# A chunked recurrence with a block-row solver in place of a power-series solver, followed by a capacity-dropping expert layer

## The chip, the cores and the metric

The kernel runs on one core of one Trainium2 chip, in one launch. The metric is device time in microseconds (us), the median of several runs; lower is better. Before the change it is 1976.67 us, the median of 3 runs (1975.95 to 1977.36).

## The reference

```python
# attention: batch 4, heads 8, tokens 768, head size 40, all float32
for t in range(S):
    y[:, :, t] = einsum('bhd,bhde->bhe', r_t, state)
    Sa = einsum('bhde,bhe->bhd', state, a_t)
    state = state * w_t[:, :, None, :] - einsum('bhd,bhe->bhde', Sa, b_t)
    state = state + einsum('bhd,bhe->bhde', v_t, k_t)
# experts: x = y as (3072 tokens, 320); 8 experts, hidden 1024, capacity 80
expert = argmax(x @ w_gate); gate = softmax(x @ w_gate)[expert]
for e in range(8):        # an expert keeps the 80 tokens with the greatest gates
    out[tok] = gate[tok] * (relu(x[tok] @ w1[e]) @ w2[e])
```

## The kernel before

Part 1 is the recurrence. Each token decays the state by w, so with P the running product of w from a start point, G = S / P obeys a recurrence without decay: G_t = G_{t-1} + v_t kh_t' + u_t nb_t', u_t = G_{t-1} ah_t, with ah = a times the product before t, kh = k / P, nb = -b / P. Within a stretch of tokens the u are the solution of a triangular system, U = (I - N)^-1 (ah G_0 + Psi V).

A unit is 128 tokens of one batch with all 8 heads; there are 24 units (6 chunks of 128 tokens times 4 batches). Two heads share 128 partitions, padded from 40 to 64 each. Inside a unit the products restart every 32 tokens (C = 32, NS = 4 sub-chunks); the masks `before` and `after` are block-diagonal in 32 tokens.

`prepare(n)` does what needs no state: six loads on the SP queue (`load`), transposes through TensorE (`transposed`, L180), the running product on VectorE (L225), its reciprocal (L229), the products N, its transpose, Psi and Lambda (`scores`, L192 with the mask at L199), and the inverse. The inverse is the product (I + N)(I + N^2)(I + N^4)(I + N^8)(I + N^16): a `while` loop multiplies z by a factor on TensorE (L264 by way of L192) and adds it on VectorE (L267), and squares N and its transpose (`power`, L192, copied by ScalarE at L208). `finish(n)` does what needs the state: for each of 4 sub-chunks a transposed copy of the state (L305), u (L309, L311), and the state step (L318, L320, L323, L324); then Lambda of u, y (L340 to L349), the token rows of x and the logits.

`together(finish(n), prepare(n + 1))` takes a step of each in turn, so the two generators' instructions alternate in each engine's queue. Each engine runs its queue in order; a framework places the instructions and puts semaphores between engines.

An f32 matmul stands in the trace as two passes, each a weight load and a MATMUL; a transpose is one pass. After every fourth unit `gate` picks experts and merges the greatest gates with 10 rounds of MAX8 and MATCH_REPLACE8 on VectorE. Part 2 (L429 on) finds each expert's tokens and runs the 8 experts; it starts when part 1 ends.

Of the kernel before, what the change touches and what calls it, by code (L numbers as in the profile page):

```python
# [8 lines left out]
F32 = mybir.dt.float32  # L9
# [4 lines left out]
Alu = mybir.AluOpType  # L14
PSUM = bass.MemoryType.PSUM
# [3 lines left out]
def kernel(  # L19
# [57 lines left out]
    def keep(o, i, op, base, pattern, cm):  # L77
# [18 lines left out]
    own = const.tile([128, 1, 1, 2], F32, name="own")
    nc.vector.memset(own, 0.0)
    nc.vector.memset(own[0:HB, :, :, 0:1], 1.0)
    nc.vector.memset(own[HB:128, :, :, 1:2], 1.0)
    # E, E - 1, ... 1: the greatest of those at the maxima is the first maximum  # L100
# [4 lines left out]
    # a tile m = (ci, batch) holds tokens batch * S + ci * T + p; one more than that  # L105
# [31 lines left out]
    with ExitStack() as p1:  # L137
        hold = p1.enter_context(tc.tile_pool(name="hold", bufs=1))
        sb = p1.enter_context(tc.tile_pool(name="sb", bufs=2))
        ps_t = p1.enter_context(tc.tile_pool(name="ps_t", bufs=2, space=PSUM))  # L140
        ps_s = p1.enter_context(tc.tile_pool(name="ps_s", bufs=2, space=PSUM))
        ps_c = p1.enter_context(tc.tile_pool(name="ps_c", bufs=2, space=PSUM))
# [7 lines left out]
        src = dict(w=w, a=a, k=k, b=b, r=r, v=v)  # L150
        raw = {n: padded(f"raw_{n}", 3 if n == "v" else 2, [128, H, HB], 1.0 if n == "w" else 0.0) for n in src}
        decay = padded("decay", 2, [128, G * NS, C], 0.0)
        u_t = padded("u", 2, [128, H, HB], 0.0)
        state = [padded(f"state{i}", 2, [128, G, 2, HB], 0.0) for i in range(B)]
# [7 lines left out]
        def given(name, n):  # L162
            return raw[name][n % len(raw[name])]

        def load(n):
            if n >= len(units):
                return
            ci, bi = units[n]
            for name, ap in src.items():
                nc.sync.dma_start(given(name, n)[:, :, 0:D],  # L170
                                  ap[bi, :, ci * T : (ci + 1) * T, :].rearrange("h t d -> t h d"))
# [4 lines left out]
        def transposed(t, n=G):  # L176
# [6 lines left out]
        def per_head(lhs, rhs, n=128):  # L183
            """A product per head, heads of parity q in bank q: index (q, g)."""
            p = ps_s.tile([128, 2, 512], F32, name="sp", tag="s")
            for g in range(G):
                for q in range(2):
                    o = p[:, q, g * n : (g + 1) * n]
                    x = rhs(q, g)
                    if len(x.shape) == 3:  # L190
                        o = o.rearrange("p (s d) -> p s d", s=x.shape[1])
                    nc.tensor.matmul(o, lhsT=lhs(q, g), rhs=x, start=True, stop=True)  # L192
            return p

        def scores(lhs, rhs, mask, tag, bufs):
            p = per_head(lambda q, g: lhs[HB * q : HB * q + D, g, :],
                         lambda q, g: rhs[HB * q : HB * q + D, g, :])
            o = sb.tile([128, 2, G, 128], F32, name=tag, tag=tag, bufs=bufs)
            nc.vector.tensor_tensor(  # L199
                out=o.rearrange("p q g t -> p (q g) t"), in0=p.rearrange("p q (g t) -> p (q g) t", g=G),  # L200
                in1=mask.to_broadcast([128, H, 128]), op=Alu.mult)
            return o

        def power(x, y, tag):
            """The square of y, of which x is the transpose."""
            p = per_head(lambda q, g: x[:, q, g, :], lambda q, g: y[:, q, g, :])
            o = sb.tile([128, 2, G, 128], F32, name=tag, tag=tag, bufs=2)
            nc.scalar.copy(o.rearrange("p q g t -> p q (g t)"), p)  # L208
            return o

        def flat(t):
            return t.rearrange("p g t -> p (g t)")

        ready = {}

        def prepare(n):
            """What needs no state, in steps."""
            rw = {name: given(name, n) for name in src}

            # running products of w, tokens along the free axis  # L220
            wp = transposed(pairs(rw["w"])).rearrange("p g (c t) -> p (g c) t", c=NS)
            dec = decay[n % 2]
            nc.scalar.copy(dec[:, :, 1:C], wp[:, :, 0 : C - 1])
            Ee = sb.tile([128, G * NS, C], F32, name="Ee", tag="Ee")
            nc.vector.tensor_tensor_scan(flat(Ee), flat(dec), flat(begins), 0.0, op0=Alu.mult, op1=Alu.add)  # L225
            Pp = sb.tile([128, G * NS, C], F32, name="Pp", tag="Pp", bufs=1)
            nc.vector.tensor_tensor(out=Pp, in0=wp, in1=Ee, op=Alu.mult)
            iP = sb.tile([128, G, 128], F32, name="iP", tag="iP", bufs=1)
            nc.vector.reciprocal(flat(iP), flat(Pp))  # L229
# [358 lines left out]
```

## Time and profile before

| | |
|---|---|
| median of 3 runs | 1976.67 us |
| profiled execution, span | 1975.8 us |
| TensorE matmul busy | 1795.4 us (91%) |
| VectorE, ScalarE, GpSimd busy | 670.5, 350.4, 32.3 us |
| mean granted TensorE clock | 0.790 |

The profiled execution's own time is its span: the first instruction starts at 0 and the last ends at 1975.8. The granted clock is a share of full speed (2.4 GHz); it has two levels, 1.0 and 0.5, so 0.79 is a mix of both in time. PE is TensorE, PEld its weight loads, DVE VectorE, ACT ScalarE, POOL GpSimd; SPq is a queue that issues DMAs. A bracket in a timeline row says how long the engine idled before the row and what released it.

### The profile page before, as it was taken

The numbers are of one execution on the slowest core, as the hardware profiler recorded it, in microseconds if no ns is written. First come the engines' busy times: TensorE is split into PE (matmuls) and PEld (weight loads), VectorE is DVE, ScalarE is ACT, GpSimd is POOL, SyncE is SP. The second block draws the span as 40 slices with busy tenths as digits, with TensorE's granted clock in tenths as the row PEclk, the third lists the DMA queues.
The fourth block names the chain that finished last, engine by engine and source line by source line (L and its number), as shares of the span: only waits on it lengthen the run. The fifth ranks groups of instructions, "written<-read, shape, count | busy, mean of one in ns | idle before, by whom it ended". The sixth has DMA issues, their size and how long they took to land. (4 is left out here: it accounts for less than half of the span.)

```text
span 1975.8 us, 28976 instructions
## 1 busy us (share of the span) xinstructions
PE 1795.4 (91%) x13014; PEld 1603.5 (81%) x13014; DVE 670.5 (34%) x1203; ACT 350.4 (18%) x503; POOL 32.3 (2%) x81
## 2 busy tenths in 40 slices
PE   4899999899999899999899999899999899982998
PEld 3798898798889789889789889789889888872766
DVE  4323323523332532332532332532332532316000
ACT  0221121121121121121121121121122112110000
POOL 1000000000000000000000000000000000000100
PEclk9886897797797797797697788788788689765677
DMA  8100100100110110110110110110110100005330
GB/s 190 17 5 17 21 8 14 34 14 11 17 21 4 31 21 4 18 21 4 31 21 4 18 21 4 31 21 4 18 21 5 34 4 1 1 1 175 121 117 7
DMA packets 168494, 55.95 MB, mean 28 GB/s; under 512 B 150964, under 2 KB 165556, under 8 KB 168372
## 3 DMA queue, kind: packets, MB, share of 16 engines
q1 hardware_dynamic: 160896, 44.58, 11.0%
q10 hardware_dynamic: 6708, 7.89, 1.2%
q8 instruction: 103, 1.69, 0.3%
q0 software_dynamic: 768, 1.64, 0.3%
q14 instruction: 19, 0.16, 0.0%
HBM read 45.40 MB, written 8.70 MB: 27 GB/s over the span
## 5 line engine op out<-in xcount | busy, mean ns | idle before, releaser
L192 PE MATMUL sp<-z,Nt 128*128 128x80 f32 x1920 | 281.4, 308 | 1.8 <-ACT Nt L208 1.2
L192 PEld LDWEIGHTS sp<-z,Nt 128*128 128x128 f32 x1920 | 261.9, 219 | 16.8 <-issue 6.4
L192 PE MATMUL sp<-Nt,Nn 128*128 128x128 f32 x1536 | 228.3, 311 | 0.0
L192 PEld LDWEIGHTS sp<-Nt,Nn 128*128 128x128 f32 x1536 | 217.6, 226 | 0.0
L208 ACT COPY Nt<-sp 128x1024 f32<-128x1024 f32 x96 | 97.2, 1012 | 489.9 <-PE sp L192 489.9
L318 PE MATMUL cp<-raw_v,kh 32*128 32x80 f32 x736 | 171.4, 318 | 0.0
L267 DVE TENSOR_TENSOR z<-sp,z 128x320 f32<-128x320 f32 x240 | 106.6, 486 | 189.9 <-PE sp L192 189.9
L320 PE MATMUL cp<-u,nb 32*128 32x80 f32 x736 | 165.7, 310 | 3.9 <-DVE u L311 3.9
L323 DVE TENSOR_TENSOR acc<-cp,state 128x320 f32<-128x320 f32 x92 | 43.9, 477 | 313.0 <-PE cp L320 313.0
L318 PEld LDWEIGHTS cp<-raw_v,kh 32*128 32x128 f32 x736 | 132.7, 223 | 17.2 <-issue 11.9
L192 PE MATMUL sp<-Nn,Nt 128*128 128x128 f32 x1152 | 141.2, 276 | 0.0
L305 ACT COPY sd<-tp 128x512 f32<-128x512 f32 x96 | 56.4, 587 | 478.7 <-PE tp L180 477.2
L320 PEld LDWEIGHTS cp<-u,nb 32*128 32x128 f32 x736 | 134.2, 225 | 5.0 <-DVE u L311 4.8
L192 PEld LDWEIGHTS sp<-Nn,Nt 128*128 128x128 f32 x1152 | 135.9, 194 | 0.0
L311 DVE TENSOR_TENSOR u<-cp,z 32x320 f32<-32x320 f32 x96 | 46.7, 486 | 215.0 <-PE cp L309 214.9
L192 PE MATMUL sp<-ahT,nbT 40*128 40x128 f32 x384 | 49.9, 437 | 65.7 <-DVE nbT L240 65.7
L309 PE MATMUL cp<-state,zT 128*32 128x80 f32 x768 | 108.0, 291 | 0.0
L340 PEld LDWEIGHTS tp<-rT,sd 128*128 128x128 f32 x768 | 96.3, 197 | 12.8 <-issue 12.8
L340 PE MATMUL tp<-rT,sd 128*128 128x32 f32 x768 | 104.4, 281 | 0.0
L192 PEld LDWEIGHTS sp<-ahT,nbT 40*128 40x128 f32 x384 | 42.8, 324 | 72.4 <-DVE nbT L240 72.4
L309 PEld LDWEIGHTS cp<-state,zT 128*32 128x32 f32 x768 | 74.0, 139 | 31.2 <-issue 30.3
L542 PE MATMUL hp<-xe,w 128*128 128x80 f32 (+1 forms) x384 | 87.6, 374 | 1.4 <-DVE xe L534 1.4
(181 smaller groups left out, 2054.5 us busy)
## 6 DMA issues: line engine op xcount, KB each, us to landing
w<-in_moe_w_dram SPq DMA_DIRECT2D x8, 1280.0 KB, 8.8
w<-in_moe_w_dram SPq DMA_DIRECT2D x8, 1024.0 KB, 5.6
x_rows<-xb ACTq DMA_DIRECT2D x6, 642.0 KB, 4.2
out_dram<-zero ACTq DMA_DIRECT2D x8, 480.0 KB, 5.5
raw_w<-in_w_dram SPq DMA_DIRECT2D x24, 160.0 KB, 3.2
raw_a<-in_a_dram SPq DMA_DIRECT2D x24, 160.0 KB, 3.5
raw_k<-in_k_dram SPq DMA_DIRECT2D x24, 160.0 KB, 3.3
raw_b<-in_b_dram SPq DMA_DIRECT2D x24, 160.0 KB, 3.2
```

The lines of the kernel that those rows point to most:

```text
L192: nc.tensor.matmul(o, lhsT=lhs(q, g), rhs=x, start=True, stop=True)
L208: nc.scalar.copy(o.rearrange("p q g t -> p q (g t)"), p)
L267: nc.vector.tensor_tensor(out=zq, in0=p[:, q, 0 : G * 2 * D].rearrange("p (g s d) -> p g s d", g=G, s=2), in1=zq, op=Alu.add)
L305: nc.scalar.copy(sd, transposed(old.rearrange("p g q d -> p g (q d)")))
L309: nc.tensor.matmul(pu[tt, 2 * g : 2 * g + 2, :], lhsT=zT[:, g, tt], rhs=old[:, g, :, 0:D], start=True, stop=True)
L311: nc.vector.tensor_tensor(out=u[tt, :, 0:D], in0=pu[tt], in1=z[tt, 1, :, 0:D], op=Alu.add)
L318: nc.tensor.matmul(pg[:, g], lhsT=pairs(kh)[tt, g, :], rhs=rv[tt, h2, 0:D], start=True, stop=False)
L320: nc.tensor.matmul(pg[:, g], lhsT=pairs(nb)[tt, g, :], rhs=u[tt, h2, 0:D], start=False, stop=True)
L323: nc.vector.tensor_tensor(out=acc, in0=pg, in1=old[:, :, :, 0:D], op=Alu.add)
L340: nc.tensor.matmul(yp[:, g, tt], lhsT=starts[c][:, g, :], rhs=rT[:, g, tt], start=c == 0, stop=False, skip_group_check=True)
L542: nc.tensor.matmul(hp[:, f - f0, :], lhsT=w1[:n, i, f * 128 : (f + 1) * 128], rhs=xe[:n, i, :], start=i == 0, stop=i == len(KB) - 1)
```

## The change

The running products now run over all 128 tokens, and there is one state per batch, stepped once per unit. The system of 128 tokens is solved by block rows of 32: row c subtracts what the earlier rows contribute (L298), and multiplies by the inverse of its own diagonal block (L302). The 32x32 diagonal blocks of four units (4 batches x 4 blocks x 8 heads = 128 matrices) are written to DRAM, read back with one matrix in each partition, inverted there on VectorE by 30 steps of two instructions, written to DRAM and read back as weights (`invert`, once per four units). Preparation runs 5 units ahead, and the generators are gone: `finish(n)` is written out whole, then `prepare(n + 5)`. The products that divide b and k by P, and two of the masks, go to GpSimd (POOL). `gate` and part 2 stay as they are; comments are gone, so line numbers shift.

```diff
-        def power(x, y, tag):          # squares, ScalarE copies
-            while j < C:               # five factors, z += N^j z
-            for c in range(NS):        # in finish: 4 state steps a unit
-        together(finish(n, xb, lg), prepare(n + 1))
+        def by_pool(p, o):
+            nc.scalar.copy(o.rearrange("p q g t -> p (q g t)"), p.rearrange("p q g t -> p (q g t)"))
+            oo = o.rearrange("p q g t -> p (q g) t")
+            nc.gpsimd.affine_select(out=oo, in_=oo, compare_op=Alu.is_gt, fill=0.0, base=0,
+                                    pattern=[[0, H], [1, 128]], channel_multiplier=-1)
+        def prepare(n):
+            load(n, early)
+            nc.scalar.copy(dec[:, :, 1:], transposed(pairs(raw_w)))
+            nc.vector.tensor_tensor_scan(flat(pt), flat(dec), flat(begins), 0.0, op0=Alu.mult, op1=Alu.add)
+            nc.vector.scalar_tensor_tensor(out=ahT, in0=transposed(pairs(raw_a)), scalar=-1.0,
+                                           in1=pt[:, :, 0:T], op0=Alu.mult, op1=Alu.mult)
+            nc.vector.reciprocal(ip, heads(transposed(pt[:, :, 1:])))
+            nc.gpsimd.tensor_tensor(out=ub[:, :, 0:D], in0=raw_b[:, :, 0:D], in1=ip, op=Alu.mult)
+            nc.gpsimd.tensor_tensor(out=kh[:, :, 0:D], in0=raw_k[:, :, 0:D], in1=ip, op=Alu.mult)
+            ubT = copied("ubT", pairs(ub))
+            by_vector(scores(ubT, ahT), nt)
+            for c in range(NS):
+                nc.sync.dma_start(blocks[k, bi, c].rearrange("h (s t) -> s h t", s=C),
+                                  nt[tt].rearrange("p q g t -> p (q g) t")[:, :, tt])
+        def invert(k):
+            nc.sync.dma_start(lt, blocks[k].rearrange("b c h x -> (b c h) x"))
+            nc.scalar.copy(tt, lt)
+            for s in range(1, C - 1):
+                n = C - 1 - s
+                nc.vector.tensor_tensor(
+                    out=tm, in0=t3[:, 0:s, s : s + 1].to_broadcast([128, s, n]),
+                    in1=l3[:, s : s + 1, s + 1 :].to_broadcast([128, s, n]), op=Alu.mult)
+                nc.vector.tensor_tensor(out=t3[:, 0:s, s + 1 :], in0=t3[:, 0:s, s + 1 :], in1=tm, op=Alu.add)
+            nc.sync.dma_start(solved[k].rearrange("b c h x -> (b c h) x"), tt)
+            for bi in range(B):
+                for c in range(NS):
+                    nc.sync.dma_start(dt_[c * C : (c + 1) * C].rearrange("p q g t -> p (q g) t"),
+                                      solved[k, bi, c].rearrange("h (s t) -> s h t", s=C))
+        def finish(n, xb, lg):
+            by_pool(scores(copied("khT", pairs(kh), 1), ahT), lam)
+            by_pool(scores(vT, rT), lamv)
+            ...
+            for c in range(NS):
+                for h in range(H if c else 0):
+                    nc.tensor.matmul(pr[tt, h, :], lhsT=nt[0 : c * C, h % 2, h // 2, tt], rhs=u[0 : c * C, h, 0:D],
+                                     start=False, stop=True, skip_group_check=True)
+                nc.scalar.copy(yy[tt], pr[tt])
+                for h in range(H):
+                    nc.tensor.matmul(pu[tt, h, :], lhsT=dt_[tt, h % 2, h // 2, :], rhs=yy[tt, h, :],
+                                     start=h == 0, stop=True, skip_group_check=True)
+                nc.vector.tensor_copy(u[tt, :, 0:D], pu[tt])
+            ...
+        for ci in range(NCI):
+            for bi in range(B):
+                finish(n, xb, lg)
+                if m < len(units):     # m = n + AHEAD, 5
+                    prepare(m)
+                    if m % B == B - 1:
+                        invert(m // B)
```

On TensorE, in the middle of a unit before the change, the squares and factors of the next unit (Nt, Nn, z) stand between the steps of this one (u, sd, lamv, rT):

```order
L192 MATMUL sp<-Nt,Nn 128x128 x8
L180 MATMUL tp<-ident,u_144 128x128 x4
L340 MATMUL tp<-rT,sd 128x32 x4
L344 MATMUL tp<-lamv,kh 64x128
L192 MATMUL sp<-rT,uT 128x128 x8
L192 MATMUL sp<-z,Nt 128x80 x8
L346 MATMUL tp<-lamu,nb 64x128
```

After the change, the same place in a unit holds the last two of that unit's block rows (pu from dt, pr from nt) and then its end:

```order
L302 MATMUL pu<-yy,dt 32x40 x8
L298 MATMUL pr<-u_164,nt 32x40 x8
L302 MATMUL pu<-yy,dt 32x40 x8
L311 MATMUL pg<-u_164,ub_152 64x80 x8
L182 MATMUL tp<-ident,u_164 128x128 x4
L328 MATMUL yp<-rT,gT 128x128 x3
L196 MATMUL sp<-rT,uT 128x128 x8
L328 MATMUL yp<-rT,gT 128x128
L333 MATMUL yp<-lamv,kh_140 64x128 x8
L333 MATMUL yp<-lamu,ub_152 64x128 x8
L182 MATMUL tp<-ident,xT 128x128 x4
```

What stood between a unit's dependent steps there, another unit's matmuls, is no longer in that place.

On TensorE, at the seam between two units before the change, the preparation (raw_b, raw_k, nbT, ahT, khT) has state steps of the running units (u, nb, state, zT) among it:

```order
L320 MATMUL cp<-u_143,nb 128x80
L180 MATMUL tp<-ident,raw_b_126 128x128 x4
L180 MATMUL tp<-ident,raw_k_122 128x128 x4
L192 MATMUL sp<-ahT,nbT 128x128 x8
L192 MATMUL sp<-nbT,ahT 128x128 x8
L180 MATMUL tp<-ident,state_156 128x128 x4
L309 MATMUL cp<-state_156,zT 32x80 x4
L192 MATMUL sp<-ahT,khT 128x128 x8
```

After the change the end of a unit (xT, lp) is followed by the preparation of the unit five later (raw_w to ub_156), and that by the start of the next unit (kh_140):

```order
L182 MATMUL tp<-ident,xT 128x128 x4
L341 MATMUL lp<-wg,xT 128x8 x4
L182 MATMUL tp<-ident,raw_w_112 128x128 x4
L182 MATMUL tp<-ident,raw_a_116 128x128 x4
L182 MATMUL tp<-ident,pt 128x128 x4
L182 MATMUL tp<-ident,ub_156 128x128 x4
L182 MATMUL tp<-ident,kh_140 128x128 x4
L196 MATMUL sp<-ahT,ubT 128x128 x8
L196 MATMUL sp<-ahT,khT 128x128 x8
L182 MATMUL tp<-ident,raw_r_128 128x128 x4
```

The transposes that wait for the running product (pt) and its reciprocal (ub) now stand one behind the other, with one group of transposes (raw_a) before the first and none between the two.

On VectorE before the change, a unit's u and end (lamu) stand among the next one's factors (z):

```order
L311 TENSOR_TENSOR u_144<-cp,z 32x8x40
L267 TENSOR_TENSOR z<-sp,z 128x4x2x40 x2
L323 TENSOR_TENSOR acc<-cp,state_160 128x320
L324 TENSOR_TENSOR state_159<-acc,ends 128x8x40
L267 TENSOR_TENSOR z<-sp,z 128x4x2x40 x2
L199 TENSOR_TENSOR lamu<-sp,before 128x1024
```

After the change, the last steps of an inverse (tmp, tt) stand between the gate's rounds (MAX, MATCH_REPLACE on cand), in front of the next unit's u:

```order
L256 TENSOR_TENSOR tmp<-tt,lt 128x58
L378 MAX cand_180<-cand_179 128x8
L259 TENSOR_TENSOR tt<-tt,tmp 128x29x2
L379 MATCH_REPLACE cand_179<-cand_180,cand_179 128x208
L256 TENSOR_TENSOR tmp<-tt,lt 128x30
L378 MAX cand_180<-cand_179 128x8
L259 TENSOR_TENSOR tt<-tt,tmp 128x30
L379 MATCH_REPLACE cand_179<-cand_180,cand_179 128x208
L304 COPY u_163<-pu 32x8x40 x4
L315 TENSOR_TENSOR acc<-pg,state_167 128x320
```

The inverse of units 4k to 4k+3 ends right before unit 4k starts on its block rows.

## Rows read from the trace of the kernel before

**Rows 1.** The page, part 1: busy us, share of the span, instructions.

```profile
PE 1795.4 (91%) x13014; PEld 1603.5 (81%) x13014; DVE 670.5 (34%) x1203; ACT 350.4 (18%) x503; POOL 32.3 (2%) x81
```

**Rows 2.** Stretches: length, busy and count of PE, PEld, DVE, ACT, POOL; clock, DMA.

```profile
310.20:381.90 71.70, 66.46 (x506) 60.22 (x505) 30.49 (x72) 13.93 (x21) 0.68 (x3) 0.81 0.11 24
445.90:473.30 27.40, 24.12 (x135) 22.09 (x136) 11.23 (x15) 1.76 (x3) 0.00 (x0) 0.51 0.08 13
1747.00:1785.00 38.00, 32.31 (x164) 27.59 (x164) 5.69 (x11) 2.77 (x5) 0.00 (x0) 0.50 0.00 0
1798.00:1976.00 178.00, 149.52 (x591) 107.86 (x589) 25.85 (x71) 7.00 (x16) 14.96 (x16) 0.65 0.36 113
```

**Rows 3.** Timeline of one unit's preparation: start, us, engine, line, idle before.

```profile
449.18 2.08 PE L192 MATMUL sp<-ahT,nbT 40*128 40x128 f32 x16 [3.54 <-DVE nbT L240]
```

**Rows 4.** Timeline, last unit of part 1 alone on TensorE.

```profile
1747.07 1.09 PE L180 MATMUL tp<-ident,state 128*128 128x128 f32 x4 [1.27 <-DVE state L324]
1748.08 1.28 PE L309 MATMUL cp<-state,zT 128*32 128x80 f32 x8
...
1765.61 1.75 PE L340 MATMUL tp<-rT,sd 128*128 128x32 f32 x8
...
1767.91 2.08 PE L192 MATMUL sp<-rT,uT 40*128 40x128 f32 x16
...
1774.22 0.70 PE L344 MATMUL tp<-lamv,kh 128*64 128x128 f32 x4
1774.70 0.65 PE L346 MATMUL tp<-lamu,nb 128*64 128x128 f32 x4
...
1782.87 1.72 PE L357 MATMUL lp<-wg,xT 128*128 128x8 f32 x8
```

**Rows 5.** Groups by line and form: busy us, mean ns; idle before, releaser.

```profile
L192 PE MATMUL sp<-z,Nt 128*128 128x80 f32 x1920 | 281.4, 308 | 1.8 <-ACT Nt L208 1.2 <-DVE z L260 0.7
L318 PE MATMUL cp<-raw_v,kh 32*128 32x80 f32 x736 | 171.4, 318 | 0.0
L208 ACT COPY Nt<-sp 128x1024 f32<-128x1024 f32 x96 | 97.2, 1012 | 489.9 <-PE sp L192 489.9
L229 DVE RECIPROCAL iP<-Pp 128x512 f32<-128x512 f32 x24 | 80.2, 3340 | 0.0
L311 DVE TENSOR_TENSOR u<-cp,z 32x320 f32<-32x320 f32 x96 | 46.7, 486 | 215.0 <-PE cp L309 214.9
L199 DVE TENSOR_TENSOR lamu<-sp,before 128x1024 f32<-128x1024 f32 x24 | 29.4, 1224 | 104.5 <-PE sp L192 104.5
L225 DVE TENSOR_TENSOR_SCAN Ee<-decay,begins 128x512 f32<-128x512 f32 x24 | 29.3, 1220 | 15.1 <-ACT decay L223 15.1
L394 DVE MAX8 cand<-cand 128x8 f32<-128x208 f32 x60 | 21.7, 361 | 0.8
L349 DVE TENSOR_TENSOR xT<-tp,Ee 128x512 f32<-128x512 f32 x24 | 16.6, 691 | 119.5 <-PE tp L346 119.5
L331 ACT COPY uT<-tp 128x512 f32<-128x512 f32 x24 | 14.2, 592 | 2.4 <-PE tp L180 2.4
L354 ACT COPY xb<-tp 128x320 f32<-128x320 f32 x24 | 10.2, 426 | 55.4 <-PE tp L180 55.4
```

**Rows 6.** The same of GpSimd alone.

```profile
L232 POOL TENSOR_TENSOR ends<-Pp,own 128x32 f32<-128x32 f32 x24 | 5.7, 239 | 1327.3 <-DVE Pp L227 1327.3
...
L78 POOL TENSOR_SCALAR_AFFINE_SELECT strict<-ones 128x128 f32<-128x128 f32 x1 | 0.3, 282 | 0.0
```

**Rows 7.** Timeline of TensorE at the program's start.

```profile
21.38 1.08 PE L180 MATMUL tp<-ident,raw_w 128*128 128x128 f32 x4 [21.38 <-DMA raw_w<-in_w_dram]
...
38.05 3.61 PE L258 MATMUL cp<-raw_v,psi 128*128 128x40 f32 x16 [0.33 <-issue]
```

**Rows 8.** The page, part 6: DMA issues, KB each, us to landing.

```profile
out_dram<-zero ACTq DMA_DIRECT2D x8, 480.0 KB, 5.5
```

**Rows 9.** Timeline of VectorE where part 1 ends.

```profile
1784.62 0.17 DVE L358 COPY lg<-lp 128x8 f32<-128x8 f32 x1 [2.72 <-PE lp L357]
```

More of the change, by code (lines that the diff above doesn't have):

```diff
@@ L148, in padded @@
             return ts
[L150 to L154, printed above, removed]
+        early = dict(w=w, a=a, k=k, b=b)
+        late = dict(r=r, v=v)
+        raw = {n: padded(f"raw_{n}", 2, [128, H, HB], 1.0 if n == "w" else 0.0) for n in (*early, *late)}
+        decay = padded("decay", 2, [128, G, T + 1], 0.0)
+        khs = padded("kh", NK, [128, H, HB], 0.0)
+        ubs = padded("ub", NK, [128, H, HB], 0.0)
+        us = padded("u", 2, [128, H, HB], 0.0)
+        state = padded("state", B, [128, G, 2, HB], 0.0)
         og_t = padded("og", 2, [128, B, 32], 0.0)
@@ L181, in transposed, with copied, scores @@
             return p
-        def per_head(lhs, rhs, n=128):
-            p = ps_s.tile([128, 2, 512], F32, name="sp", tag="s")
+        def copied(name, t, bufs=2):
+            o = sb.tile([128, G, 128], F32, name=name, tag=name, bufs=bufs)
+            nc.scalar.copy(o, transposed(t))
+            return o
+        def scores(lhs, rhs):
+            p = ps_s.tile([128, 2, G, 128], F32, name="sp", tag="s")
             for g in range(G):
                 for q in range(2):
[L188 to L192, printed above, removed]
-            return p
@@ L204, in power @@
-        def power(x, y, tag):
[L206 to L214, printed above, removed]
+                out=o.rearrange("p q g t -> p (q g) t"), in0=p.rearrange("p q g t -> p (q g) t"),
+                in1=before.to_broadcast([128, H, 128]), op=Alu.mult)
@@ L226, in prepare @@
[L226 to L229, printed above, removed]
-            ends = sb.tile([128, NS, G, 2], F32, name="ends", tag="ends")
-            nc.gpsimd.tensor_tensor(
-                out=ends, op=Alu.mult, in1=own.to_broadcast([128, NS, G, 2]),
-                in0=Pp[:, :, C - 1 : C].rearrange("p (g c) o -> p c g o", c=NS).to_broadcast([128, NS, G, 2]))
@@ L243, in prepare @@
-            nc.vector.tensor_tensor(out=khT, in0=transposed(pairs(rw["k"])), in1=iP, op=Alu.mult)
-            yield
-            Nt = scores(nbT, ahT, before, "Nt", 2)
-            Nn = scores(ahT, nbT, after, "Nn", 2)
-            yield
-            psi = scores(khT, ahT, before, "psi", 1)
-            z = sb.tile([128, 2, H, HB], F32, name="z", tag="z")
-            nc.scalar.copy(z[:, 0].rearrange("p (g q) d -> p g (q d)", q=2), transposed(ahT))
-            yield
-            pv = ps_c.tile([128, H, D], F32, name="cp", tag="c")
@@ L292, in finish @@
         def finish(n, xb, lg):
             ci, bi = units[n]
-            Eg, ends, z, zT, kh, nb, rT, lamv = ready.pop(n)
-            rv = given("v", n)
-            u = u_t[n % 2]
-            starts = []
+            pt, ahT, ub, kh, nt = made.pop(n)
+            dt_ = inverse.pop((ci, bi))
+            load(n, late)
+            rr, rv = raw["r"][n % 2], raw["v"][n % 2]
+            st = state[bi]
+            lam = sb.tile([128, 2, G, 128], F32, name="psi", tag="psi", bufs=1)
+            by_pool(scores(copied("khT", pairs(kh), 1), ahT), lam)
@@ new lines, in finish @@
+            lamu = sb.tile([128, 2, G, 128], F32, name="lamu", tag="lamu", bufs=1)
+            by_vector(scores(copied("uT", pairs(u), 1), rT), lamu)
+            yp = ps_t.tile([128, G, 128], F32, name="yp", tag="t")
+            for g in range(G):
+                nc.tensor.matmul(yp[:, g, :], lhsT=gT[:, g, :], rhs=rT[:, g, :],
+                                 start=g == 0, stop=False, skip_group_check=True)
+            for x, y in ((kh, lamv), (ub, lamu)):
+                for g in range(G):
+                    for q in range(2):
+                        nc.tensor.matmul(yp[HB * q : HB * (q + 1), g, :], lhsT=x[:, 2 * g + q, :], rhs=y[:, q, g, :],
+                                         start=False, stop=x is ub, skip_group_check=True)
@@ L356, in finish @@
+            xT = sb.tile([128, G, 128], F32, name="xT", tag="xT")
+            nc.vector.tensor_tensor(out=xT, in0=yp, in1=pt[:, :, 0:T], op=Alu.mult)
+            nc.scalar.copy(xb[:, bi, 0:DM].rearrange("p (h d) -> p h d", h=H), heads(transposed(xT)))
+            lp = ps_t.tile([128, E], F32, name="lp", tag="t")
             for g in range(G):
```

208 lines of the change are left out of this document (79 added, 129 removed).

## The prediction, made before the changed kernel ran

> **What bounds the kernel now.** I read the page first. TensorE is busy for 91% of the span, in 13014 passes; VectorE and ScalarE are far below [rows 1]. So I asked for a table of stretches. A unit of part 1 takes 71.7 us, holds 506 recorded passes, and TensorE is busy 66.5 us of it, at a mean clock of 0.81 [rows 2]. The reader is to see that the bound is TensorE's own work, and that its price has two levels: 27.4 us of each period run at half clock (1.2 of 2.4 GHz) and hold 135 passes, about 0.2 us each [rows 2]. The timeline shows what comes before the fall: TensorE idles 3.54 us, until VectorE has the reciprocal and the product behind it [rows 3]. The last unit of part 1 has no other unit beside it. It shows how a unit runs alone: from 1747 to 1785 TensorE is busy 32.3 of 38 us, with gaps such as 1.27 us, and the clock is 0.50 throughout [rows 2, 4]. That stretch is my model of the changed kernel. Part 1 ends with the last logits at 1784.8 [rows 9]; what follows takes 1975.8 - 1784.8 = 191 us and is not changed.
>
> **What goes.** The power series goes: 5 factors and 7 squares of 8 matmuls each, 12 x 8 x 2 = 192 passes a unit. So do 3 of 4 state steps and transposed states. By the order, a unit has 320 passes afterwards (40 transposes; 64 of scores; 16 + 8 + 32 + 64 + 48 + 8 + 32 + 8 others), against the 506 recorded before. At the old mean price this alone would take the unit from 71.7 to 71.7 x 320/506 = 45 us. But the other unit that stood between dependent steps goes too, so a unit costs its chain of waits, and I price the chain.
>
> **Which clock.** The seam has two idle stretches per unit. The transposes of w and a take 1.8 us, while the decay copy and the scan need 0.6 + 1.2 us behind the first [rows 5], so TensorE idles about 1.3 us. Then it waits for the reciprocal of 320 columns, 3.34 x 320/512 = 2.1 us [rows 5], and for GpSimd's product, about 3 us in all. Waits of 3.5 and of 1.3 us stood before half-clock stretches in the trace [rows 3, 4]. I price all of part 1 at half clock.
>
> **Prices at half clock.** A transpose is 0.22 us (1.09 for four with 0.2 of latency at the end), a score pass 0.117 (2.08 for 16), a pass with 128 columns of weights 0.21 to 0.22 (L340, L357, L258), a pass with 64 columns 0.105 (eight from 1774.22 to 1775.35, less 0.3 of latency) [rows 4, 7]. A hand-over between engines is 0.05 to 0.15.
> No row has a pass of 32 columns of weights and 40 columns of data (L302, L298; 112 a unit). The nearest is L309: 32 columns of weights, 80 of data, 1.28 us for 8, which is 0.28 + 7 x 0.14 [rows 4]. If the data columns set it, half of them give 0.07; if not, 0.14. I take 0.09, nearer the half, and 1.6 us for 16.
> A rule weighs on this term. Contracting 32 rows instead of 128 buys nothing in the rows: 318 ns for L318 against 308 for z [rows 5]. The Trainium skill, TensorE: Matmul & The Clock Gate, section "Why this matters for your kernels", says the same, and that small blocks gain only when they run beside each other in different tiles of the array; here each block row waits for the one before. By that rule the block height buys nothing and 0.14 would stand, which is the second rival below.
> GpSimd has no row of these sizes. A select over 1024 columns lies between ScalarE's copy of as many, 1.0 us, and 8 x 0.282 = 2.3 [rows 5, 6]; taking 0.1 as its fixed part I use 1.5. A product of 320 columns lies between VectorE's 0.49 and 0.1 + 320 x (0.239 - 0.1)/32 = 1.5 [rows 5, 6]; I use 0.8.
> The Trainium skill, GPSIMD Engine Reference, section "Elementwise — side-by-side cycle accounting", has two-input work there about twice as slow as on VectorE. By that the product would be an estimated 0.97 us and the sum 4 us more.
>
> **One unit, in four parts.**
> A, preparation: transposes of w 1.1, decay copy 0.6, scan 1.25, transposes of pt 1.1, reciprocal 2.1, GpSimd 0.8, transposes of ub and kh 1.8, two groups of scores 3.9, hand-overs 0.5: 13.1 us.
> B, to the right-hand side: copy 1.0 and select 1.5 with hand-overs, 2.75 (three groups of transposes, 2.6, lie under it); 2 passes of L286 0.44; scores 1.86; 14 passes 3.1; 8 of L289 1.76; latency 0.3: 10.2 us.
> C, block rows: kh.v, which the order puts ahead of the first L302, 1.5; four L302 6.4; three L298 4.8; four copies of u 2.0 and three of yy 1.3 [rows 5]; eleven hand-overs 1.3: 17.3 us.
> D, end: ub.u 1.5, transposes 0.9, six passes of L328 1.3, scores 1.86, two more and 32 passes of L333 with latency 4.1, xT 0.85, transposes 1.1, logits 1.76: 13.4 us. VectorE's state step and lamu (1.22) lie under L333.
> Sum: 54 us. TensorE's share in it is 42 (the same prices over its 320 passes), so the chain is the bound. The last four units have no preparation and no state step: 39.5 us each.
>
> **The inverse.** 60 VectorE instructions, 9920 columns in all. VectorE takes 0.486 us for 320 and 1.224 for 1024 [rows 5], so 0.15 + 1.05 ns a column: 9.0 + 10.4, say 20 us. It is hidden only as far as a unit lasts. In order, its last 21 steps (6.2) alternate with the gate's 20 (at MAX8's 0.361 [rows 5], with their loads 8.0) and stand behind nt and before the next u: 15.5 us with overhead. Then the matrices go out, for which I take the 5.5 us of a 480 KB store [rows 8], and 32 KB pieces come back, 0 to 5.5, I take 3. So 24 us lie between nt and the first L302, where the other path needs 12: 12 us of stall, four times; the fifth time there is no preparation as cover, and it is 19. Sum: 67 us. SP issues the returning pieces in order behind the store, and later loads of r, v, w stand behind them; those are two units ahead, and cost nothing while the stall stays below a unit.
>
> **The start.** The first transposes come at 21.4 [rows 7]. Four preparations, each 9.5 behind the last, the last one whole: 42. Out to DRAM 3, back 5.5 (bounds as above), copy 1, inverse 20 with nothing beside it, out and back 8.5: first block row at 101. Chain and end of unit 0: 29.
>
> **Sum.** 101 + 29 + 19 x 54 + 4 x 39.5 + 67 + 191 = 1572. It is made against the profiled span of 1975.8, 0.9 under the median; I predict **1570 us**.
>
> **Rivals.**
> 1. The clock comes back in each unit's dense end (scores and L333, 7 us without a wait). For it: the clock does return in every period of the trace, after 27 us [rows 2]. Against it: that return follows dense full-width matmuls, and D is followed at once by the idle seam. D and what is left of A at full clock save about 6 us a unit: 1572 - 23 x 6 = 1430. If the clock stays up through most of part 1, a unit is about 37 us, and the time 1200.
> 2. Small passes cost 0.14: 112 x 0.05 = 5.6 us a unit, 24 times: 1705. For it the K = 32 rows above; against it the fewer data columns.
> 3. The other side: small passes do not follow each other closely, because all eight of a group stand in one 32x32 corner of the array and write one strip of PSUM. One pass alone has 0.28 to 0.3 of latency; unpipelined, 112 x (0.31 - 0.09) = 25 us a unit, 24 times 590: 2160, slower. It decides from 404/(24 x 112) = 0.15 us above my price, 0.24 a pass. Against it: L309 and L318 pipeline [rows 4, 5].
> 4. The inverse decides: at the price of 320 columns each, 60 x 0.486 = 29 us, 9 more at the start and in each stall: 1572 + 54 = 1625, inside my range.
>
> **How the numbers follow.** My sum 0.50, rival 4 0.06, rival 1 0.20 (its strong form 0.04 more), rival 2 0.15, rival 3 0.04, unnamed 0.01. Range 1430 to 1710: it holds the sum, rivals 2 and 4 and most of rival 1. A measurement of this kernel tells about 0.2%, 4 us, from no change. Faster 0.95, same 0.01, slower 0.04, the last from rival 3.
>
> **What would show it.** Right: clock near 0.5 over part 1; units about 54 us apart; TensorE's idle time named by GpSimd, VectorE's reciprocal and the u and yy copies; groups of L302 at 1.6 us; before units 4, 8, 12, 16, 20 a wait for dt of 12 to 19 us. Wrong: a clock above 0.7 in part 1; L302 groups at 2.4 us or at 5; no wait for dt, or one that outlasts a unit.

## The result, and the profile after

The changed kernel takes 1302.35 us (median of four runs, 1299.19 to 1305.5) against 1976.31 for the kernel before, run beside it: a ratio of 0.659, 95% interval 0.658 to 0.660. The forecast was 1570 us with a range of 1430 to 1710. The direction is right, the size is not: the gain is 674 us where 407 were forecast. The profiled execution has a span of 1303.7 us. Medians and ranges, here and below, leave out executions more than 1.5% above the fastest of their kernel: 1308.0 and 1314.4 us with all waits filled, 1542.1 in the interleaved kernel with the same fills, 1385.4 in the changed kernel with wider data, and 4166.1 in the kernel before, run beside that one.

The first part of the page, to be read beside [rows 1], and the row of the granted clock:

```profile
PE 958.8 (74%) x8150; PEld 815.8 (63%) x8150; DVE 440.5 (34%) x1015; ACT 211.0 (16%) x365; POOL 128.2 (10%) x179
...
PEclk9966775668566767775677656675765567557777
```

TensorE's passes fall from 13014 to 8150 and its share of the span from 91% to 74%: it now waits in every unit, as foreseen. But its clock in part 1 is not 0.5; it moves between 0.5 and 0.8. Next the stretches, as in [rows 2]: two whole units (5 and 6, counting from 0), then the four parts of unit 7: preparation, right-hand side, block rows, end.

```profile
301.40:343.20 41.80, 32.45 (x320) 28.64 (x320) 10.31 (x14) 8.19 (x14) 4.06 (x5) 0.71 0.16 28
343.20:390.10 46.90, 38.12 (x320) 33.54 (x320) 10.32 (x13) 8.19 (x14) 4.06 (x5) 0.56 0.14 25
390.10:402.40 12.30, 7.51 (x53) 6.49 (x54) 5.31 (x4) 1.76 (x3) 1.68 (x2) 0.69 0.32 55
402.40:409.00 6.60, 6.60 (x54) 6.13 (x56) 0.00 (x0) 3.75 (x5) 2.18 (x2) 0.81 0.48 124
409.80:421.40 11.60, 8.15 (x114) 7.00 (x114) 3.76 (x12) 2.30 (x4) 0.15 (x1) 0.58 0.09 16
421.40:431.50 10.10, 8.75 (x88) 7.65 (x88) 8.20 (x23) 1.01 (x2) 0.22 (x1) 0.80 0.01 2
```

A unit holds the 320 passes that were counted from the order, and lasts 42 to 47 us, not 54. Both units do the same work; the one of 46.9 us had the lower clock, 0.56 against 0.71. Inside unit 7 the clock is low in the preparation and the block rows, where TensorE is busy 61% and 70% of the time, and high in the right-hand side and the end (100% and 87%). The timeline of TensorE shows the turns:

```profile
390.13 0.66 PE L182 MATMUL tp<-ident,raw_w 128*128 128x128 f32 x4 [0.26 <-DVE lg L342]
...
392.73 0.66 PE L182 MATMUL tp<-ident,pt 128*128 128x128 f32 x4 [1.51 <-DVE pt L223]
396.64 1.12 PE L182 MATMUL tp<-ident,ub 128*128 128x128 f32 x4 [3.25 <-POOL ub L230]
...
398.54 2.08 PE L196 MATMUL sp<-ahT,ubT 40*128 40x128 f32 x16
400.41 1.92 PE L196 MATMUL sp<-ahT,khT 40*128 40x128 f32 x16
...
405.18 1.16 PE L196 MATMUL sp<-rT,vT 40*128 40x128 f32 x16
...
409.79 0.76 PE L302 MATMUL pu<-yy,dt 32*32 32x40 f32 x16
...
412.39 1.27 PE L302 MATMUL pu<-yy,dt 32*32 32x40 f32 x16 [0.51 <-ACT yy L300]
414.24 1.27 PE L298 MATMUL pr<-u,nt 64*32 64x40 f32 x16 [0.57 <-DVE u L304]
...
426.73 1.09 PE L333 MATMUL yp<-lamv,kh 128*64 128x128 f32 x16
...
460.28 0.97 PE L302 MATMUL pu<-yy,dt 32*32 32x40 f32 x12 [6.29 <-DMA dt<-solved]
```

Four transposes take 0.66 us ahead of the wait of 3.25 us and 1.12 behind it; sixteen score passes take 2.08 at half clock, and 1.16 after 8 us of work without a wait. A group of sixteen small passes takes 0.76 us at full clock and 1.27 at half. The last row is the wait for the diagonal inverse, in unit 8. Eight us without a wait do not always bring the clock back. In unit 6 the same passes run without a wait from 350.5 to 368.6 us, at half clock all the time:

```profile
350.49 1.11 PE L182 MATMUL tp<-ident,ub 128*128 128x128 f32 x4 [3.25 <-POOL ub L230]
...
359.22 2.08 PE L196 MATMUL sp<-rT,vT 40*128 40x128 f32 x16
...
367.40 1.27 PE L302 MATMUL pu<-yy,dt 32*32 32x40 f32 x16
```

What TensorE waits for in all (us, times, longest; the 18.9 is the wait for the first inverse, ahead of unit 0):

```profile
PE tp L182 <- POOL ub L230: 77.5, 24, 3.3
PE pu L302 <- DMA dt<-solved: 53.8, 6, 18.9
PE pu L302 <- ACT yy L300: 38.2, 75, 0.6
PE pr L298 <- DVE u L304: 36.1, 68, 0.6
PE tp L182 <- DVE pt L223: 26.0, 19, 1.6
```

And the groups that had no row before, to be held against the estimates from [rows 5, 6] (busy us, mean ns):

```profile
L228 DVE RECIPROCAL ip<-tp 128x320 f32<-128x320 f32 x24 | 51.8, 2158 | 3.5 <-PE tp L182 2.9
L207 POOL TENSOR_SCALAR_AFFINE_SELECT psi<-psi 128x1024 f32<-128x1024 f32 x24 | 27.0, 1127 | 221.7 <-ACT psi L205 221.7
L230 POOL TENSOR_TENSOR ub<-raw_b,ip 128x320 f32<-128x320 f32 x24 | 20.7, 861 | 308.8 <-DVE ip L228 308.8
L259 DVE TENSOR_TENSOR tt<-tt,tmp 128x30 f32<-128x30 f32 (+9 forms) x180 | 64.9, 361 | 3.8
L256 DVE TENSOR_TENSOR tmp<-tt,lt 128x30 f32<-128x30 f32 (+9 forms) x180 | 61.5, 341 | 4.0 <-ACT tt L248 1.2
```

### The profile page after: what moved, and what is told of

It reads as the page before. It is cut to its first block, busy times and chain, and to the rows that moved or that the text cites. A ratio compares the mean times of both kernels' runs of the same rounds, so it can differ in the third digit from the quotient of the medians.

```text
span 1303.7 us, 19040 instructions
## 1 busy us (share of the span) xinstructions
PE 958.8 (74%) x8150; PEld 815.8 (63%) x8150; DVE 440.5 (34%) x1015; ACT 211.0 (16%) x365; POOL 128.2 (10%) x179
## 5 line engine op out<-in xcount | busy, mean ns | idle before, releaser
L302 PE MATMUL pu<-yy,dt 32*32 32x40 f32 x1536 | 109.4, 247 | 92.1 <-DMA dt<-solved 53.8
L302 PEld LDWEIGHTS pu<-yy,dt 32*32 32x32 f32 x1536 | 95.0, 148 | 106.0 <-issue 55.4
L298 PE MATMUL pr<-u,nt 64*32 64x40 f32 (+2 forms) x1152 | 81.3, 248 | 36.5 <-DVE u L304 36.1
L298 PEld LDWEIGHTS pr<-u,nt 64*32 64x32 f32 (+2 forms) x1152 | 70.5, 149 | 48.0 <-DVE u L304 48.0
L524 PEld LDWEIGHTS hp<-xe,w 128*128 128x128 f32 (+1 forms) x384 | 73.2, 256 | 16.5 <-DVE xe L516 1.9
L259 DVE TENSOR_TENSOR tt<-tt,tmp 128x30 f32<-128x30 f32 (+9 forms) x180 | 64.9, 361 | 3.8
L256 DVE TENSOR_TENSOR tmp<-tt,lt 128x30 f32<-128x30 f32 (+9 forms) x180 | 61.5, 341 | 4.0 <-ACT tt L248 1.2
L286 PEld LDWEIGHTS pr<-raw_v,psi 128*128 128x128 f32 x384 | 56.5, 227 | 4.5 <-issue 1.1
L286 PE MATMUL pr<-raw_v,psi 128*128 128x40 f32 x384 | 59.2, 312 | 0.1
L228 DVE RECIPROCAL ip<-tp 128x320 f32<-128x320 f32 x24 | 51.8, 2158 | 3.5 <-PE tp L182 2.9
L196 PEld LDWEIGHTS sp<-ahT,ubT 40*128 40x128 f32 x384 | 42.9, 325 | 10.9 <-ACT ubT L187 10.9
```

Source lines behind the costliest of these rows:

```text
L196: nc.tensor.matmul(p[:, q, g, :], lhsT=lhs[m, g, :], rhs=rhs[m, g, :], start=True, stop=True)
L228: nc.vector.reciprocal(ip, heads(transposed(pt[:, :, 1:])))
L256: nc.vector.tensor_tensor(out=tm, in0=t3[:, 0:s, s : s + 1].to_broadcast([128, s, n]), in1=l3[:, s : s + 1, s + 1 :].to_broadcast([128, s, ...
L259: nc.vector.tensor_tensor(out=t3[:, 0:s, s + 1 :], in0=t3[:, 0:s, s + 1 :], in1=tm, op=Alu.add)
L286: nc.tensor.matmul(pr[:, h, :], lhsT=lam[:, h % 2, h // 2, :], rhs=rv[:, h, 0:D], start=h == 0, stop=False, skip_group_check=True)
L298: nc.tensor.matmul(pr[tt, h, :], lhsT=nt[0 : c * C, h % 2, h // 2, tt], rhs=u[0 : c * C, h, 0:D], start=False, stop=True, skip_group_check ...
```

## Where the 268 us between forecast and measurement lie

The parts are read from the end of VectorE's copy of each unit's logits, TensorE's first and last pass of a group, and VectorE's last copy of u. Fifteen of the units 1 to 19 have no wait for dt; four have.

| term | forecast | measured | difference |
| --- | --- | --- | --- |
| start to the first block row | 101 | 97.5 | -4 |
| unit 0, block rows and end | 29 | 22.8 | -6 |
| 15 units: A 13.1, B 10.2, C 17.3, D 13.4 | 54 | 12.5 + 7.5 + 12.0 + 10.9 = 42.9 | 15 x -11.1 = -167 |
| 4 units with the wait for dt | 66 | 51.1 | 4 x -14.9 = -60 |
| last four units, with their wait | 177 | 146.1 | -31 |
| what follows part 1 | 191 | 189.8 | -1 |

The units that ran at half clock through their first three parts (3, 6, 15, 18) split the 11.1 us: A 13.0, B 10.0, C 13.9 with what stands ahead of it, and D 12.0 in the units with the lowest clock there (0.63). Against these the average unit is 0.5 + 2.5 + 1.9 + 1.1 = 6 us shorter: that is the clock. The other 5 us are prices: 3.4 of them in C, 1.4 in D (where no unit with a state step ran wholly at half clock, so part of the 1.4 may still be clock).

## Experiments

**The wait between units, filled.** The waits for pt and for ub are filled with dummy matmuls whose results are overwritten:

```
+            for i in range(fill):          # transposed(pt, 5), transposed(ub, 12)
+                nc.tensor.matmul(p[:, i % G, :], lhsT=ident, rhs=ones, start=True, stop=True)
             for g in range(G):
                 nc.tensor.transpose(p[:, g, :], t[:, g, :], ident)
```

> The changed kernel with dummy 128x128 matmuls put on TensorE ahead of two sets of transposes of each prepared unit: 5 ahead of those of pt (it waits 1.38 us there) and 12 ahead of those of ub (3.22 us). Their results are overwritten; nothing else is changed. Theory (the clock): the granted clock falls to 0.5 because of these two waits between units, and the chain of block rows then runs at half clock. With the waits filled the clock stays up: chain 12.7 -> about 10.3 us in every unit, right-hand-side part 6.6 us in every unit, unit 41.8 -> 38 to 39 us, the time 1302 -> about 1235 us, mean granted clock in the units above 0.8 instead of 0.67. Rival A: the clock does not answer to these waits; the dummies only fill idle time, no change within 0.5%. Rival B: the dummies delay the transposes behind them, +1.5 us a unit, about 1335 us.

Measured: 1250.1 us (1244.0 to 1251.2), ratio to before 0.632 (0.630 to 0.634): 52 us less than the changed kernel, with more work on TensorE. The parts of unit 2 (preparation, right-hand side, block rows, end):

```profile
154.30:164.20 9.90, 9.16 (x87) 8.06 (x88) 4.93 (x4) 1.66 (x3) 1.68 (x2) 1.00 0.40 68
164.20:170.60 6.40, 5.75 (x54) 5.03 (x56) 0.33 (x1) 3.59 (x5) 2.18 (x2) 1.00 0.30 49
171.20:181.80 10.60, 7.15 (x116) 6.06 (x114) 1.90 (x4) 1.25 (x3) 0.00 (x0) 0.72 0.10 17
181.80:191.80 10.00, 8.93 (x88) 7.84 (x88) 3.08 (x6) 1.01 (x2) 0.20 (x1) 0.78 0.00 0
```

The clock is 1.00 through the first two parts, so with these two waits filled it no longer falls there. In the block rows it falls all the same: their mean over units 1 to 19 is 11.6 us against 11.5, where the expectation had 10.3. That part of it was wrong, and the time came out 15 us above it. The four units that wait for dt gained nothing: what their preparation saves, the wait takes back (9.0 us instead of 6.1), and they take 51.4 us as against 51.1, while the other fifteen fall from 42.9 to 39.3.

**The same in the kernel before.** My step took the half clock of [rows 2, 3] over to the new kernel as if one wait decided it. Sixteen dummy matmuls ahead of the scores of nbT and ahT fill that wait.

> The kernel before, with 16 dummy 128x128 matmuls (32 passes, results overwritten) put on TensorE ahead of the scores of nbT and ahT, where it waits 3.54 us for the reciprocal and the product behind it in every unit. Theory: the 27 us at half clock of every unit of 71.7 us follow from that one wait. With the wait filled the granted clock stays at full speed; half of 27 us less is some 12 to 14 us a unit, 24 units: 1976 -> 1650 to 1720 us, mean clock in a unit above 0.95 instead of 0.81. Rival A: the half clock has another cause (what TensorE runs there, or a fixed share): no change or, by the dummies' own time, +0 to +2 us a unit, 1976 to 2025 us.

Measured: 1826.8 us (1818.1 to 1830.3), ratio 0.923 (0.920 to 0.926). The right direction, half the size. Two stretches, the high one and the low one that follows:

```profile
222.00:232.80 10.80, 10.80 (x56) 10.17 (x55) 2.85 (x6) 0.59 (x1) 0.00 (x0) 0.53 0.00 0
168.00:222.00 54.00, 53.22 (x495) 48.71 (x494) 21.53 (x30) 13.66 (x19) 0.24 (x1) 1.00 0.12 19
```

The low stretch shrinks from 27.4 us [rows 2] to some 10 and now begins behind the passes of 32 rows (L320, L322 here) and in those of 40 data columns (L260), while TensorE is busy without a pause. So filling the wait takes away most of the half clock of the kernel before, and something that is not a wait makes the rest.

**All waits filled.** Two dummies more ahead of each group of small passes but a unit's first, two ahead of ub.u and three ahead of the transposes of xT, on top of the first experiment.

> The changed kernel with the dummies of e1 and, in the chain of block rows, two dummy 128x128 matmuls (0.245 us each at full clock) ahead of each group of small passes, where TensorE waits 0.51 to 0.59 us for the copies of yy and u, and three ahead of the transposes of xT (0.80 us). Their results are not used. Theory: the clock falls inside the chain because of these waits; filled, it stays at full speed in the whole unit: preparation 9.9, right-hand side 6.5, chain 9.6 to 10 instead of 10.6 to 12.7, end 8.6 to 9 instead of 10 to 12, unit about 35.5 us instead of 37.6 to 41.4 in e1: 1250 -> 1165 to 1185 us. Rival: the small passes themselves do not hold the clock and it falls all the same; then the dummies cost twice their time, 0.98 us for two in a wait of 0.5: +0.5 us in seven places, unit 41 to 43 us, 1260 to 1310 us.

Measured: 1283.3 us (1277.6 and 1288.9), 33 us more than with two waits filled. Each theory holds in a part of the units. Of units 1 to 19, eight kept the clock and take 35.3 to 35.9 us (9.9 + 6.5 + 0.6 + 9.6 + 8.8): that is what a unit costs at full clock, dummies included. In the other eleven it fell, and they take 45.6 to 54.6 us, four of them with the wait for dt. One high and the next low stretch:

```profile
273.80:331.80 58.00, 54.34 (x595) 46.83 (x593) 17.67 (x20) 13.72 (x24) 7.72 (x9) 1.00 0.23 37
331.80:355.60 23.80, 23.80 (x197) 20.72 (x198) 2.93 (x6) 2.25 (x5) 0.42 (x2) 0.50 0.05 8
```

The fall at 331.8 us comes in the passes of 40 and 80 data columns of the right-hand side (L289, L292), with no wait over 0.63 us in the 15 us ahead of it, and the low stretch lasts although TensorE is busy in all of it. In it the dummies cost 1.22 us in waits of 0.5, and what the full units gained is spent.

**The small pass, priced in place.** Every group of L302 is issued twice (`for h in [*range(H), *range(H)]`).

> The changed kernel with each group of 8 small passes (32 tokens by 32) by the diagonal inverse issued twice, the second time with the same result: 64 passes... of 16 passes a group 16 more, in four groups a unit, 24 units. It prices the small pass where it runs. Theory: 0.066 us at half clock and 0.04 at full clock, +2.6 to 4.2 us a unit, the time 1302 -> 1375 to 1400 us (if a pass of f32 counts as two instructions, 64 more a unit). By the prediction's 0.09 us: +138 us, 1440. By its bound of 0.14: +215, 1517. Rival: passes hide behind the copies, under +20 us.

Measured: 1384.2 us (1366.9 to 1385.7), ratio 0.698 (0.693 to 0.703): +82 us, the theory's size. At half clock:

```profile
290.60 1.27 PE L298 MATMUL pr<-u,nt 32*32 32x40 f32 x16 [0.57 <-DVE u L304]
292.38 2.33 PE L302 MATMUL pu<-yy,dt 32*32 32x40 f32 x32 [0.51 <-ACT yy L300]
```

(2.33 - 1.27)/16 = 0.066 us a pass, and 0.28 of latency once a group (0.28 + 15 x 0.066 = 1.27). At full clock:

```profile
338.53 0.76 PE L298 MATMUL pr<-u,nt 32*32 32x40 f32 x16 [0.29 <-DVE u L304]
339.79 1.33 PE L302 MATMUL pu<-yy,dt 32*32 32x40 f32 x32 [0.51 <-ACT yy L300]
```

(1.33 - 0.76)/16 = 0.036 us a pass. The forecast's 0.09 and its bound of 0.14 are both refuted.

**Preparation between the block rows.** The function that prepares a unit becomes a generator with three yields, and the chain of unit n takes a step of unit n+5 behind each copy of yy:

```
                 nc.scalar.copy(yy[tt], pr[tt])
+                next(more, None)
...
-                finish(n, xb, lg)
+                more = prepare(m) if m < len(units) else iter(())
+                finish(n, xb, lg, more)
+                list(more)
```

> The changed kernel with the preparation of unit n+5 no longer after the end of unit n, but in three pieces between the four block rows of unit n (the code order alone is changed). Theory (the unit is a chain in which TensorE mostly waits for the other engines): preparing takes 12.2 us in the row of a unit, 5 to 6 us of them waits, and the chain of block rows has some 5 us of waits of its own; laid side by side they save about 8 to 10 us of a unit, 19 units: 1302 -> 1120 to 1150 us, with the granted clock higher in the chain. Rival A: the scan, the reciprocal (2.16 us) and ScalarE's copies (about 1 us each) stand ahead of the chain's own small copies on VectorE and ScalarE and stretch it by as much as is saved: 1260 to 1310 us. Rival B: everything is in order and the units are bound by TensorE's own work: no change within 1%.

Measured: 1208.7 us (1206.4 to 1210.7), ratio 0.612 (0.610 to 0.613): 94 us less, between theory and rival A. A unit (the seventh) of this kernel:

```profile
324.70:365.40 40.70, 38.63 (x320) 33.32 (x320) 10.23 (x14) 8.77 (x15) 4.06 (x5) 0.58 0.21 41
```

Beside the unit of 41.8 us above: the same 320 passes, TensorE busy 95% instead of 78% of the time, but at 0.58 instead of 0.71. Most of the waits are gone, as the theory had it; that the clock would be higher in the chain was wrong. Where a unit kept it in the first parts, it took 34.8 us. The wait for dt is left only ahead of unit 0: the blocks of unit n+5 now leave while the chain of unit n still runs and not behind it, and the inverse ends 1.2 us behind the logits of the last unit before it is needed, where it ended 24 us behind them.

**Filling what waits are left there.** With the dummies of the kernel above with all waits filled, in the chain and at the end of this one:

> The kernel of e3 (preparation in pieces between the block rows) with the same two dummy matmuls ahead of each group of small passes and three ahead of the transposes of xT. Theory: in e3 three units of four run their first 30 us at half clock (unit 40.7 to 43.7 us), one at full clock in part (34.8 us); if the fills keep the clock up in the chain, all units take 31 to 34 us: 1209 -> 1040 to 1090 us. Rival: the clock stays at half in the chain, where TensorE is already busy 92% of the time, and 19 dummies add up to 0.49 us each, +6 to 9 us a unit: 1320 to 1380 us.

Measured: 1302.1 us (1294.6 to 1306.4), ratio 0.658 (0.655 to 0.661), 93 us more than without. The rival's direction: the clock's mean over the whole execution is 0.69, against 0.68 without, and the dummies (17 a unit by the code, not 19) are paid for. Then only the wait ahead of the transposes of xT, and in another kernel also the one behind the logits:

> The kernel of e3 (preparation in pieces between the block rows) with three dummy 128x128 matmuls (0.245 us each at full clock) ahead of the transposes of xT at the end of a unit, where TensorE waits 0.80 us; results overwritten. In e3 the clock is up at the end of a unit and falls in three units of four just behind this wait and the narrow logits. Theory: with this wait filled the clock holds through the next unit's transposes, scores and right-hand side (5.7 us instead of 9.2, and 0.9 less ahead of it) and through a part of the chain: a unit 40.7 -> 34.8 us, which is what e3's unit takes where the clock holds; 15 units of 20: 1209 -> 1120 to 1140 us. Rival A: the fall does not come from the wait but from the narrow passes in the next unit (40 columns of data, 32 rows), as in e7 and e8 where it came with no wait over 0.65 us ahead: the fall moves by a few us at most, 1195 to 1215 us. Rival B: the clock falls earlier in turn, or the chain lengthens: over 1220.

> As e9, with four more dummy matmuls ahead of the transposes of kh, directly behind the logits (8 columns of data) of the unit before, where TensorE waits 0.26 us for the copy of the logits. They take 0.98 us at full clock and 1.95 at half, so at least 0.7 us of every unit is spent. Theory: the clock holds into the chain of every unit, and the unit is 35.5 to 36 us against 40.7 in e3: 1120 to 1150 us. Rival: the narrow passes let it fall all the same, and the dummies cost 0.7 to 1.7 us a unit: 1225 to 1250 us.

Measured: 1206.1 us (1202.2 to 1208.3) and 1208.5 (1206.0 to 1210.7), the same as without within the runs' spread. Rival A for the first. For the second neither theory nor rival came out: over units 1 to 19 the right-hand side is 2.1 us shorter in the mean than without dummies (6.2 against 8.3), and the rest of the unit, dummies included, 1.6 longer. The first one's timeline from the filled wait to the fall:

```profile
358.08 0.66 PE L184 MATMUL tp<-ident,xT 128*128 128x128 f32 x4 [0.15 <-DVE xT L342]
...
364.00 1.16 PE L198 MATMUL sp<-rT,vT 40*128 40x128 f32 x16 [0.63 <-ACT vT L189]
365.09 2.47 PE L291 MATMUL pr<-raw_v,psi 128*128 128x40 f32 x16
367.36 1.98 PE L294 MATMUL pr<-state,ahT 128*128 128x80 f32 x8
```

The fall is no longer within a microsecond or so of the logits but 7 us behind them, at 366.4 us, again in the passes of 40 data columns.

**Wider data.** So the chain and the right-hand side were fed the zero padding of their tiles: 64 data columns instead of 40 (`rhs=u[0 : c * C, h, :]` for `rhs=u[0 : c * C, h, 0:D]`, and so in the other three groups, with pr, pu and yy that wide), once in the interleaved kernel and once in the changed kernel itself.

> The kernel of e9 with every pass of the right-hand side and of the block rows fed the zero padding of its data too: 64 data columns a head instead of 40 (128 instead of 80 for the state's). The result is the same. Theory (the clock falls behind passes that are narrow in data, with no wait ahead): fed wider, they hold it; right-hand side 5.7 us in every unit and the chain near full clock, where a group of 16 passes of 64 columns would take about 1.1 us instead of 1.27 at half clock with 40: unit 37.5 to 43 -> 32 to 35 us, 1206 -> 1080 to 1130 us. Rival: the clock falls all the same (by the 32 or 96 rows or for another cause) and only the price is seen: a pass's price goes with its data columns, 0.067 x 64/40 = 0.107 us at half clock, a group 1.27 -> 1.88, seven groups +4.3 us a unit and the copy of yy +0.2 four times: 1300 to 1330 us.

> The changed kernel itself with the same wider passes, without dummies and with its own order. It also prices the small pass by its data columns. Theory: where the waits between units let the clock fall they still do; if width holds it in the chain, the chain's 12.7 us at half clock become about 11 and the time stays within 1270 to 1310 us. Rival: the clock is as before and a group of 16 goes from 1.27 to about 1.88 us at half clock (0.77 to 1.1 at full), +2.5 to 4.3 us a unit and +0.7 for the copies: 1375 to 1420 us. If the price does not go with the data columns, groups stay at 1.27 us.

Measured: 1253.5 us (1245.7 to 1258.1) and 1356.9 (1354.1 to 1366.9). Both slower, by 47 and 55 us, and both less than the rival's price. A group at half clock in the second:

```profile
287.53 1.91 PE L298 MATMUL pr<-u,nt 32*32 32x64 f32 x16 [0.57 <-DVE u L304]
```

(1.91 - 0.28)/15 = 0.109 us a pass: 0.066 x 64/40 = 0.106. The price goes with the data columns. The clock was higher with the wider data, but not enough: over units 1 to 19 of the second the right-hand side took 6.7 us instead of 7.4 (clock 0.83 instead of 0.72) and never ran at half clock as a whole, while in the chain it still fell in every unit.

**The gate, later.** The gate of a chunk is issued after the second unit of the next chunk, out of the way of the inverse.

> The changed kernel with the gate of a chunk of four units (its eight and more rounds of maximum and replace on VectorE) issued after the second unit of the next chunk, so that they no longer stand between the steps of the diagonal inverses of that chunk (xb gets a second buffer, xT one instead of two). Theory: the wait for dt ahead of units 4, 8, 12, 16, 20 (6.3 us and 2 to 3 us in the preparation) ends with VectorE's last step of the inverse, which the rounds delay by about 6.5 us; without them the waits fall to 0 to 1 us: 1302 -> about 1265 to 1275 us. Rival: the wait is that of the four DMA hops and of the 16 issues of dt on the sync queue (7.7 us), and stays: no change within 0.5%. Rival B: the gate, later, delays the unit in which it now stands by as much: no change.

Measured: 1314.4 us (1308.6 to 1317.2), ratio 0.664 (0.662 to 0.667), 12 us more. The preparation in unit 8, which needs the new inverse, that in unit 10, where the gate now stands, and the right-hand side of unit 10:

```profile
436.60:449.40 12.80, 8.14 (x53) 6.79 (x54) 12.61 (x31) 1.89 (x4) 2.61 (x4) 0.53 0.48 103
527.90:542.40 14.50, 9.35 (x58) 7.47 (x59) 10.32 (x23) 2.35 (x4) 1.67 (x2) 0.67 0.35 57
542.40:551.60 9.20, 9.20 (x50) 8.50 (x52) 3.27 (x13) 3.20 (x4) 2.18 (x2) 0.50 0.10 15
```

The inverse ends 20.9 us behind the logits of unit 7, not 24.2. But the path that needs it is shorter too: its preparation falls from 15.0 to 12.8 us, because VectorE no longer stands in its way either, and the wait for dt stays at 6.0 us. Unit 8 gains 3.0 us (51.1 to 48.1), and unit 10 loses 6.7 (41.2 to 47.9), 2.6 of them in a right-hand side at half clock. The theory is refuted; rival B is right and too mild.

## Why the prediction was wrong

- **"I price all of part 1 at half clock": wrong, the largest step.** The mean clock over units 1 to 19 was 0.66: in most of them it comes back twice. This is my rival 1, which I gave 0.20, and which priced it in D and a part of A alone. It missed B: in fifteen of these units, after the two groups of scores and the transposes, the clock is up for the right-hand side (in units 3, 6, 15 and 18 it is not). The argument against it ("D is followed at once by the idle seam") held for what follows D, not for D. The model was the last unit of the kernel before, at 0.50 throughout [rows 2]; that one has the other end of a unit and no preparation. Clock: 6 of 11 us a unit. That rival 1 had 6 us too is luck, since 4.4 of the 6 lie in B and C.
- **"I take 0.09" for a small pass: too high; it is 0.066 at half clock and 0.036 at full.** [Rows 4] gave 0.14 for 80 data columns, and half the columns cost half. I held back because fewer contracted rows had bought nothing [rows 5]. At half clock, groups of L298 with 32, 64 and 96 rows all take 1.27 us, so they buy nothing here either; but that says nothing against a low price, since the pass is cheap for its data columns, not for its rows. The Trainium skill, TensorE: Matmul & The Clock Gate, section "Why this matters for your kernels", has a matmul over 32 rows take as long as one over 128; the trace agrees as far as its 32 to 96 rows go. Seven groups at 1.27 instead of 1.6 are 2.3 of the 3.4 us in C; the rest are hand-overs in the chain, counted at 0.12 each beside the copies where the rows show 0.51 and 0.57 us for copy and hand-over together, and 0.3 for kh.v.
- **The chain as the bound: right.** TensorE is busy 78% of a unit and waits where I said: ub, pt, yy, u, and dt.
- **A at 13.1: right** (12.5 on average, 13.0 at half clock), with the reciprocal at 2.16 (2.1), GpSimd's product at 0.86 (0.8) and its select at 1.13 (1.5). The estimate for the product that was worked out from the Trainium skill, GPSIMD Engine Reference, section "Elementwise — side-by-side cycle accounting", was 0.97; the measurement lies between the two.
- **The inverse: right in kind, half the size.** Sixty instructions at 0.35 us are 21 us against 20. The stall is 8.2 us a chunk, not 12, and 10.5 at the end, not 19. From nt to the first L302 of the unit behind it 16.2 us pass, not 24: the inverse ends 11.7 behind nt (forecast 15.5), and out and back take 4.5, not 8.5. The median landing times (KB each, us) in the stretch of 240 to 345 us:

```profile
solved<-tt SPq DMA_DIRECT2D x1, 512.0 KB, 2.6
dt<-solved SPq DMA_DIRECT2D x16, 32.0 KB, 1.8
```

- **Rivals 2, 3 and 4: refuted**, by the groups of 1.27 us (2 and 3) and by 0.35 us an instruction (4). Start, tail and counts were right within 5 us.

What stays open: why the clock falls where TensorE does not wait, and why the same passes brought it back in fifteen units and not in four. The runs show the fall behind passes that are narrow in data or in rows, and a higher clock with wider data; they don't show what the chip counts. Nor do they part two causes that each edit changed together: wider passes also kept TensorE busy for longer, and a dummy both fills a wait and adds wide work. The fastest kernel found is the interleaved one, 1208.7 us, 7% below the changed kernel (0.612/0.659 = 0.928); the 2.5 us that three dummies took off it can't be told from nothing.

## What to carry to other kernels

Price a unit of a chain at both clock levels and say for each stretch what TensorE did before it; a stretch of wide passes without a wait in the middle of a chain can bring the clock back, as it did in fifteen of nineteen units here. The clock's return was worth 6 of 43 us in the mean unit, 2.5 of them behind that stretch. Before filling or interleaving, look at which passes run where: with most of the waits gone and narrow passes left, TensorE was busy 95% of the time in a unit, at 0.58 of full clock instead of 0.71, and part of the gain was given back. A small pass is priced from the nearest row by its data columns: at half clock it took 0.066 us with 40, 0.109 with 64 and 0.14 with 80 [rows 4].

## What the runs showed of the hardware that was not expected

- The clock can stay at 0.50 while TensorE is busy: 23.8 of 23.8 us with all waits filled, and 28.9 of 30.8 us in the interleaved kernel with the wait at the unit's end filled:

```profile
366.40:397.20 30.80, 28.93 (x236) 24.58 (x235) 22.84 (x46) 3.43 (x7) 3.17 (x4) 0.50 0.19 31
```

- Work that computes nothing made both kernels faster: 4.3 us of it a unit (1.38 + 2.94 at full clock) in the preparation took 52 us off the changed kernel in all, and sixteen matmuls a unit took 150 us off the kernel before.
- The same group of work has three prices: sixteen small passes took 0.76 us at full clock, 1.27 at half and, with 64 data columns at half, 1.91.
